# Loading Exponential's table behind ScalarE's first two copies instead of ahead of them

## Chip, cores and metric

The kernel runs on one core of a Trainium2 chip. The metric is device time in microseconds (us), the median over runs of the same program; smaller is better.

## What is computed

Routed attention is followed by a gated feed-forward layer. Batch is 4, there are 8 heads, 768 tokens, 64 numbers a head, 16 clusters a head, and a feed-forward width of 1536. Cut to what matters, the reference is:

```python
c_n = centroids / norm(centroids)              # per head, 16 clusters
q_assign = argmax(q_n . c_n); k_assign = argmax(k_n . c_n)
mask   = q_assign[..., :, None] == k_assign[..., None, :]
scores = where(mask, scale * q k^T, -1e9)
attn   = softmax(scores)                       # scale = 1/8
x      = (attn v) as [3072, 512]
xn     = x / sqrt(mean(x*x) + 1e-6) * rms_g
out    = (silu(xn @ w_gate) * (xn @ w_val)) @ w_out
```

## The kernel before

The work is cut into eight units: a batch and half of its queries (384). Inside a unit, each of the eight heads has three steps of scores; a step is two matmuls of 128 keys by 384 queries (L348) and one Exponential over 128 by 768 on ScalarE (L352). The product with the values follows one head later (`pv`, L366); after every second head VectorE divides (L371, L373). The feed-forward layer of a unit is woven into the attention of the next.

The order on every engine is written out by hand (`manual_schedule`), and each engine runs its list strictly in that order; semaphores make it wait for the others. So a late instruction delays all that stands behind it on its engine.

The mask is made inside the score matmul. Each head's keys and queries are extended by rows that hold a one in the row of the token's own cluster (tiles `kext` and `qext`, 64 rows of numbers and 16 of clusters). For the first heads they are prepared thus, and this document calls the key and query of head n "key n" and "query n":

1. `trans(g, h, part)`: TensorE transposes the loaded float32 tile in three matmuls into PSUM (tile `tq`, L221, one of three buffers), and a copy brings it to SBUF (tile `qkT`): by ScalarE (L227), or by VectorE where `on` is `nc.vector` (L225). `part` 1 is the key, 0 the query.
2. `casts(pool_, n, ...)`: GpSimd (POOL) casts `qkT` to bfloat16 into `kext` and `qext` (L240), in halves of the tokens: K0 and K1 of the key, Q0 and Q1 of the query.
3. `pair_clusters`: TensorE multiplies with the normalised centroids (tile `cblk`) into `sc` (L320), VectorE transposes (L323, `scT`), takes the maximum (L326, `mx`) and compares (L327, `pads`).
4. `head(n)`, that is `under`: VectorE transposes the compared tile into the cluster rows (L332), key first, then query.

POOL also casts the values (`vcast`, L243, tile `vbf`) and issues the loads of the weights (L204). The beginning of POOL's list is: K0, Q0, K1 of head 0; K0, Q0, K1 of head 1; K0, K1, Q0 of head 2; the same of head 3; Q1 of heads 0 and 1; the value cast of head 0; the first two weight loads; the value cast of head 1; Q1 of heads 2 and 3; the value casts of heads 2 and 3; K0, K1, Q0 of head 4.

The beginning of TensorE's list is: key 0, the transpose of the centroids (`c_ps`, L192), query 0, key 1, the clusters of head 0, query 1, key and query 2, the clusters of head 1, key and query 3, key 4, and then the scores of head 0. The first product with the values stands behind the second score step of head 1, and behind it stand the transposes of key and query 7, a score step, and the clusters of heads 4 and 5.

The centroids' norms are made by ScalarE's Sqrt (L182), and ScalarE's functions need their table: the profile shows an ACT_TABLE_LOAD ahead of Sqrt, one ahead of the first Exponential, and one ahead of the first Silu near the end. `first_exp` (L184) is an Exponential of 128 numbers whose output nobody reads; it stands where the table is to be loaded. `off` is a constant that POOL wrote at the start.

Of the kernel before, what the change touches and what calls it, by code (L numbers as in the profile page):

```python
# [14 lines left out]
ACT = mybir.ActivationFunctionType  # L15
# [7 lines left out]
def kernel(  # L23
# [12 lines left out]
    nc = tc.nc  # L36
# [135 lines left out]
    off = const.tile([P, 1], F32)  # L172
# [8 lines left out]
    c_norm = const.tile([P, 1], F32)  # L181
    nc.scalar.activation(c_norm, c_ss, ACT.Sqrt)  # L182
    first_exp = const.tile([P, 1], F32)
    nc.scalar.activation(first_exp, off, ACT.Exp)  # L184
    c_inv = const.tile([P, 1], F32)
    nc.vector.reciprocal(c_inv, c_norm)
    nc.vector.tensor_scalar_mul(c_n[:, :D], c_in, c_inv)
# [2 lines left out]
    def centroids_t():  # L190
        c_ps = ps_s.tile([P, P], F32, tag="s", name="c_ps")
        nc.tensor.transpose(c_ps, c_n, ident_f)  # L192
        nc.vector.tensor_copy(cblk[:D, :, :NC], c_ps[:D].rearrange("d (h c) -> d h c", c=NC))
        nc.vector.tensor_copy(cblk[D:, :, NC:], c_ps[D:].rearrange("d (h c) -> d h c", c=NC))
# [17 lines left out]
    def trans(g, h, part, on=None):  # L212
        if (g, h // 2) not in qkT:
            qkT[g, h // 2] = qk32.tile([P, 2, 2, UQ], F32, tag="qkT", name="qkT")
        qk = staged[g * HG + h]
        if g * HG + h >= BH:
            nc.vector.transpose(qkT[g, h // 2][:, h % 2, part], qk[:, part].rearrange("p t d -> p (t d)"))
            return
        ps = ps_g.tile([P, UQ], F32, tag="gen", name="tq")
        for i in range(HT):  # L220
            nc.tensor.transpose(ps[:, i * P:(i + 1) * P], qk[:, part, 2 * i:2 * i + 2].rearrange("p t d -> p (t d)"),  # L221
                                ident_f)
        to, by = qkT[g, h // 2][:, h % 2, part], 1.0 / ZS if part and g < BG else 1.0
        if on is nc.vector:
            nc.vector.tensor_scalar_mul(to, ps, by)  # L225
        else:
            nc.scalar.activation(to, ps, ACT.Copy, scale=by)  # L227
# [84 lines left out]
    def pair_clusters(p, heads=(0, 1)):  # L312
        g, h = divmod(2 * p, HG)
        what = [(h + i, m) for i in heads for m in range(2)]
        at = [slot(2 * p + i, m) for i in heads for m in range(2)]
        r = slice(min(at), max(at) + 32)
        pool = ps_g if p else ps_s
        ps = pool.tile([P, UQ], F32, tag="gen" if p else "s", name="sc")
        for a, (hh, m) in sorted(zip(at, what)):
            nc.tensor.matmul(ps[a:a + 32], lhsT=cblk[:, g * HG + hh], rhs=qkT[g, hh // 2][:, hh % 2, m],  # L320
                             start=True, stop=True)
        sct = asg.tile([P, UQ], F32, tag="scT", name="scT", bufs=2)
        nc.vector.transpose(sct[r], ps[r])  # L323
        cl = sct[r].rearrange("p (b e c) -> p b e c", e=2, c=NC)
        mx = small.tile([P, NB, 2], F32, tag="mx", name="mx")[r]
        nc.vector.tensor_reduce(mx, cl, axis=AX, op=ALU.max)  # L326
        nc.vector.tensor_tensor(pads[p][r, :, :NC].rearrange("p b c e -> p b e c"), cl,  # L327
                                mx.unsqueeze(3).broadcast_to([mx.shape[0], NB, 2, NC]), op=ALU.is_equal)
# [234 lines left out]

    K0, K1, Q0, Q1 = (1, 0), (1, 1), (0, 0), (0, 1)
    pool_ = nc.gpsimd
    trans(0, 0, 1, nc.vector)
    centroids_t()
    trans(0, 0, 0)
    trans(0, 1, 1)
    pair_clusters(0, (0,))  # L570
    casts(pool_, 0, K0, Q0, K1)
# [173 lines left out]
```

## Time and profile before

| | before |
|---|---|
| median of 3 runs | 327.1 us (326.96 to 327.35) |
| profiled execution | 327.35 us, of which the span is 325.6 |
| PE (TensorE matmul) busy | 317.8 us, 98% of the span |
| ACT (ScalarE) busy | 245.6 us, 75% |
| DVE (VectorE) busy | 219.8 us, 68% |
| POOL (GpSimd) busy | 137.9 us, 42% |
| granted TensorE clock | 1.00 in every stage |

All times of instructions are in us from the start of the span. A row of the timeline gives start, duration, engine, line, operation, output<-input, shapes, the number of merged instructions and, in brackets, how long the engine had sat idle and what ended that. A row of the windows gives a stretch, its length, and for each engine its busy time and, in brackets, its instructions. The chain of waits is followed back from the end of the stretch that is asked for.

### The profile page before, as it was taken

The numbers are of one execution on the slowest core, as the hardware profiler recorded it, in microseconds if no ns is written. First come the engines' busy times: TensorE is split into PE (matmuls) and PEld (weight loads), VectorE is DVE, ScalarE is ACT, GpSimd is POOL, SyncE is SP. The second block draws the span as 40 slices with busy tenths as digits, with TensorE's granted clock in tenths as the row PEclk, the third lists the DMA queues.
The fourth block names the chain that finished last, engine by engine and source line by source line (L and its number), as shares of the span: only waits on it lengthen the run. The fifth ranks groups of instructions, "written<-read, shape, count | busy, mean of one in ns | idle before, by whom it ended". The sixth has DMA issues, their size and how long they took to land.

```text
span 325.6 us, 7766 instructions
## 1 busy us (share of the span) xinstructions
PE 317.8 (98%) x2839; PEld 190.8 (59%) x2853; DVE 219.8 (68%) x502; ACT 245.6 (75%) x424; POOL 137.9 (42%) x277
## 2 busy tenths in 40 slices
PE   8999899999999999999999999999999999999996
PEld 4546656655556655665566555665566656654654
DVE  5999977989578676878677685876265645682430
ACT  5899988977769867897778866798779868862322
POOL 6999499998726265440916257350000000000000
PEclk9999999999999999999999999999999999999999
DMA  7999995997546644561555540000700040004002
GB/s 256 372 274 226 201 178 102 162 182 147 98 74 158 133 101 74 119 155 53 98 92 127 149 113 34 6 21 1 148 2 0 2 113 34 0 2 133 15 1 97
DMA packets 90310, 34.63 MB, mean 106 GB/s; under 512 B 71968, under 2 KB 87200, under 8 KB 90272
## 3 DMA queue, kind: packets, MB, share of 16 engines
q1 hardware_dynamic: 81104, 27.84, 36.6%
q0 software_dynamic: 8880, 5.91, 10.9%
q8 instruction: 22, 0.36, 0.4%
q10 hardware_dynamic: 288, 0.39, 0.4%
q14 instruction: 16, 0.13, 0.1%
HBM read 28.61 MB, written 6.29 MB: 107 GB/s over the span
## 4 chain that ended last, share of the span: by engine, by line
PE 85%; DVE 10%; ACT 2%; issue 1%; DMA 1%; DVEq 0%; ACTq 0%
PE gate L442 18%; PE val L442 18%; PE o L467 18%; PE s L348 17%; PE acc L366 9%; PE sc L254 3%; DVE kext L332 1%; DVE qext L332 1%; DVE pads L327 1%; DMA boot<-in_centroids_dram 1%; DVE x L373 1%; PE o L478 1%; ACT pT L352 1%; DVE qkT L225 1%; DVE xn L391 1%
## 5 line engine op out<-in xcount | busy, mean ns | idle before, releaser
L352 ACT ACTIVATE pT<-s,off 128x768 bf16<-128x768 f32 x192 | 170.9, 904 | 30.9 <-PE s L348 30.1
L348 PE MATMUL s<-qext,kext 80*128 80x384 bf16 x384 | 94.9, 328 | 1.6 <-ACT pT L352 0.8
L442 PE MATMUL gate<-xnT,wg 128*128 128x384 bf16 x384 | 78.4, 326 | 0.2
L442 PE MATMUL val<-xnT,wv 128*128 128x384 bf16 x384 | 78.2, 326 | 0.0
L451 DVE SCALAR_TENSOR_TENSOR th<-th,gate 128x384 f32<-128x384 f32 x81 | 44.6, 551 | 33.6 <-ACT th L450 32.9
L467 PE MATMUL o<-wo,gvT 128*128 128x512 bf16 x262 | 66.0, 379 | 0.8
L348 PEld LDWEIGHTS <-kext 80*128 80x128 bf16 x384 | 36.4, 98 | 35.1 <-issue 7.5
L455 DVE SCALAR_TENSOR_TENSOR gvT<-th,val 128x384 bf16<-128x384 f32 x81 | 44.5, 550 | 9.4 <-PE val L442 3.9
L442 PEld LDWEIGHTS <-wg 128*128 128x128 bf16 x384 | 36.1, 97 | 23.6 <-issue 1.1
L240 POOL CAST qext<-qkT 64x384 bf16<-64x384 f32 x64 | 35.6, 563 | 32.5 <-DVE inv L371 19.2
L366 PEld LDWEIGHTS <-pT 128*128 128x128 bf16 x1152 | 43.4, 97 | 10.1 <-DVE x L373 1.0
L450 ACT ACTIVATE th<-gate 128x384 f32<-128x384 f32 x81 | 39.7, 490 | 12.3 <-PE gate L442 11.5
L442 PEld LDWEIGHTS <-wv 128*128 128x128 bf16 x384 | 35.7, 97 | 22.6 <-DMA qext<-oh 0.6
L366 PE MATMUL acc<-vbf,pT 128*128 128x65 bf16 x1152 | 45.7, 193 | 0.6 <-ACT pT L352 0.2
L467 PEld LDWEIGHTS <-gvT 128*128 128x128 bf16 x276 | 26.0, 97 | 26.1 <-issue 0.2
L297 POOL DMA_DIRECT2D qext<-oh x48 | 23.1, 492 | 29.5 <-DVE oh L286 29.5
L240 POOL CAST kext<-qkT 64x384 bf16<-64x384 f32 x58 | 31.4, 541 | 4.3 <-DVE qkT L225 2.4
L470 ACT COPY o_sb<-o 128x512 f32<-128x512 f32 x23 | 13.5, 585 | 17.6 <-PE o L467 17.6
L297 POOL DMA_DIRECT2D kext<-oh x48 | 23.1, 488 | 8.1 <-DVE oh L286 7.8
L371 DVE RECIPROCAL inv<-acc 128x6 f32<-128x6 f32 x32 | 6.0, 188 | 23.7 <-PE acc L366 23.2
L373 DVE TENSOR_TENSOR x<-acc,inv 128x384 f32<-128x384 f32 x32 | 17.8, 558 | 1.1
L453 DVE TENSOR_TENSOR gvT<-th,val 128x384 bf16<-128x384 f32 x15 | 8.2, 554 | 14.7 <-PE val L442 8.2
(79 smaller groups left out, 238.4 us busy)
## 6 DMA issues: line engine op xcount, KB each, us to landing
vs<-in_v_dram SPq DMA_DIRECT2D x32, 192.0 KB, 4.0
out_dram<-o_sb SPq DMA_DIRECT2D x23, 256.0 KB, 2.5
qk<-in_q_dram SPq DMA_DIRECT2D x72, 48.0 KB, 2.6
qk<-in_k_dram SPq DMA_DIRECT2D x72, 48.0 KB, 2.5
qk<-in_q_dram SPq DMA_DIRECT2D x14, 192.0 KB, 4.1
qk<-in_k_dram SPq DMA_DIRECT2D x12, 192.0 KB, 4.2
wg<-in_moe_w_gate_dram POOLq DMA_DIRECT2D x4, 384.0 KB, 8.9
wv<-in_moe_w_val_dram POOLq DMA_DIRECT2D x4, 384.0 KB, 10.4
```

Source lines behind the costliest of these rows:

```text
L240: on.tensor_copy(to, of)
L297: on.dma_start(out=ext[D:D + NC, h, e * UQ:(e + 1) * UQ], in_=put[g, m][32 * h + e * NC:32 * h + (e + 1) * NC])
L348: nc.tensor.matmul(ps[:, j, :w] if nt == HT else flat[:, j * w:(j + 1) * w], lhsT=cols(kext[g % 4][:KR, hh], g, kc // HT, kc % HT * P, (kc ...
L352: nc.scalar.activation(pT[u, h][:, n * i:n * i + n, :w], of, ACT.Exp, bias=off, scale=scale if g >= BG else scale * ZS)
L366: nc.tensor.matmul(acc[:, h % 2, t], lhsT=pT[u, h][:, kc, t * P:(t + 1) * P], rhs=vbf[g % 4][:, hh, kc % HT * 2 + kc // HT], start=kc == 0 ...
L373: nc.vector.tensor_tensor(dst, acc[:, :, :nt, :D], inv[:, :, :nt].unsqueeze(3).broadcast_to([P, 2, nt, D]), op=ALU.mult)
L442: nc.tensor.matmul(ps, lhsT=w[:, c, f * P:(f + 1) * P], rhs=xnT[u][:, c, :n], start=c == 0, stop=c == CC - 1)
L450: nc.scalar.activation(th, ps, ACT.Tanh, scale=0.5)
L451: nc.vector.scalar_tensor_tensor(th, th, 1.0, ps, op0=ALU.add, op1=ALU.mult)
L455: nc.vector.scalar_tensor_tensor(gvT[u][:, f, :n], gates[u], 0.5, ps, op0=ALU.mult, op1=ALU.mult)
L467: nc.tensor.matmul(outs[u], lhsT=gvT[u][:, f, t * P:(t + 1) * P], rhs=wo[:, f], start=f == 0, stop=f == FC - 1)
L470: nc.scalar.copy(o, outs[u])
```

## The change

The tiny Exponential is taken away from its place behind Sqrt and put behind query 0's `trans`. Key 0's copy, which VectorE did (L225), is done by ScalarE. ScalarE's list was: Sqrt, table load, `first_exp`, the copies of query 0, key 1, query 1, ... It is now: Sqrt, the copies of key 0 and query 0, table load, `first_exp`, the copies of key 1, query 1, ...

```diff
@@ -181,7 +181,6 @@
     c_norm = const.tile([P, 1], F32)
     nc.scalar.activation(c_norm, c_ss, ACT.Sqrt)
     first_exp = const.tile([P, 1], F32)
-    nc.scalar.activation(first_exp, off, ACT.Exp)
     c_inv = const.tile([P, 1], F32)
@@ -563,9 +562,10 @@
     pool_ = nc.gpsimd
-    trans(0, 0, 1, nc.vector)
+    trans(0, 0, 1)
     centroids_t()
     trans(0, 0, 0)
+    nc.scalar.activation(first_exp, off, ACT.Exp)
     trans(0, 1, 1)
     pair_clusters(0, (0,))
     casts(pool_, 0, K0, Q0, K1)
```

## The prediction

> **What bounds the kernel now.** I read the busy time by stretch first, to see where a delay at the start could still be lost.
>
> ```profile
> 8.00:15.00 7.00, 6.55 (x48) 3.77 (x47) 6.60 (x11) 5.90 (x13) 6.60 (x12) 1.00 1.04 370
> 36.40:40.40 4.00, 3.21 (x37) 2.02 (x35) 3.62 (x14) 4.00 (x8) 0.00 (x0) 1.00 1.21 221
> 50.00:150.00 100.00, 99.66 (x924) 60.13 (x928) 76.22 (x171) 80.97 (x144) 61.77 (x125) 1.00 0.65 126
> ```
>
> Columns: PE, PEld, DVE, ACT, POOL. From 50 on PE is full, so nothing late is made up there. In 8 to 15 DVE and POOL are busy 6.60 of 7.00 each. What the start costs is paid once, 1:1, at the end; the edit lies wholly in it. Next, ScalarE's timeline and the chain of waits to 40 us:
>
> ```profile
> 4.35 1.28 ACT L184 ACT_TABLE_LOAD   x1
> 5.65 0.20 ACT L184 ACTIVATE first_exp<-off 128x1 f32<-128x1 f32 x1
> 5.75 0.86 ACT L227 ACTIVATE qkT<-tq 128x384 f32<-128x384 f32 x2
> 7.69 1.25 ACT L227 ACTIVATE qkT<-tq 128x384 f32<-128x384 f32 x3 [1.07 <-PE tq L221]
> ```
> ```profile
> 5.85 0.40 ACT qkT L227
> 6.25 0.09 issue
> 6.34 0.85 PE sc L320 x4
> ```
>
> The chain runs through the table load to query 0's copy and the first cluster product; from 7.22 it is nearly all VectorE. Last, POOL's and PE's timelines:
>
> ```profile
> 6.97 1.28 POOL L240 CAST kext<-qkT 64x384 bf16<-64x384 f32 x2
> 8.24 0.61 POOL L240 CAST qext<-qkT 64x384 bf16<-64x384 f32 x1
> 8.92 2.10 POOL L240 CAST kext<-qkT 64x384 bf16<-64x384 f32 x3
> ...
> 13.09 1.80 POOL L240 CAST qext<-qkT 64x384 bf16<-64x384 f32 x3
> 14.95 0.50 POOL L243 CAST vbf<-vs 128x384 bf16<-128x384 f32 x1
> ```
> ```profile
> 15.51 0.71 PE L366 MATMUL acc<-vbf,pT 128*128 128x65 bf16 x18
> 17.17 0.85 PE L320 MATMUL sc<-qkT,cblk 128*32 128x384 f32 x8
> ```
>
> POOL hardly idles from 6.97 to 36.40, and its value cast ends at 15.46, 0.05 before PE's first value product. That product waits for POOL; anything that makes POOL late there makes PE late.
>
> **The table's way out of the chain: 0.** Query 0's copy starts at 5.75 behind `first_exp`. But its third transpose on PE starts at 5.44 and takes 0.27: 5.71. A copy starts 0.04 behind its transpose (7.65 to 7.69), so 5.75 again. The chain names ScalarE, but PE is late by the same amount: PE waits for the centroids (DVE L188, to 4.98). The cluster product stays at 6.34.
>
> **Key 0's copy: 0.** Key 0's transposes end at 4.80; ScalarE copies from 4.84 to 5.32 (0.48, L227). DVE loses 0.55 at 4.90 to 5.45. Its copies of `cblk` end 0.08 sooner, at 6.01, where query 0's copy ends at 6.23. DVE then idled 1.13 up to 7.22, so its saving is worth nothing.
>
> **The table's new place.** The load starts 0.02 behind query 0's copy: 6.25 to 7.53; `first_exp` 7.54; key 1's copy 0.11 behind: 7.65 to 8.13, before 6.13 to 6.62. ScalarE had 1.07 idle here and 0.65 before 9.60. Query 1 follows at 8.04 (0.39 apart as now), key 2 at 8.41; query 2's transpose needs key 1's PSUM buffer: copy 8.78 for 8.45. PE's product for head 1's clusters needs query 1: 8.59 for 8.24, ends 9.43; VectorE takes it at 10.55. Key 4's copy ends 11.19 for 10.85, and the first Exponential starts at 11.20, bound by a score that ends at 11.17. ScalarE and PE are on time again: 0. The cover is VectorE's chain, 1.1 deep at head 1's clusters, but only 0.01 at the first Exponential: what came later than reckoned there would be paid 1:1.
>
> The Trainium skill (ScalarE: Activation LUTs, What ACT_TABLE_LOAD costs) gives 1.28 us for the load and 1.38 for a drain, 2.66 per switch. Here Sqrt ended at 4.33 and `first_exp` began at 5.65, 1.32 for all, so the trace decides; by the page key 1 would come 1.4 later still, and the loss below grow by about as much.
>
> **POOL.** Its cast of key 1 starts 0.06 behind the copy (6.24 to 6.30): 8.19 for 7.65, so 0.55 late. Query 1's cast was itself held by its copy; two like halves overlap by 0.08 (13.75, 14.28), so it starts at 8.73 for 8.24: 0.48 late. This is the least POOL is behind.
>
> **Casts against compares.** POOL's casts disturb DVE's compares (L327), and the other way:
>
> ```profile
> L327 DVE TENSOR_TENSOR pads<-scT,mx x5: 604/835/853, 8.4 to 24.7; 128x384 bf16<-128x384 f32 x3, 64x384 bf16<-64x384 f32 x2
> ```
>
> Alone a compare takes 0.60. One that starts under a cast ends 0.39 behind that cast (8.86 to 9.24, 12.21 to 12.60), 0.43 behind a value cast (19.80 to 20.24). A cast that starts under a compare ends 0.45 behind it (12.26 to 13.05; 0.61 alone). Replaying the list by these rows:
> - Compare 1 (8.40): key 1's cast ends 8.80, compare 9.19 (9.24 before). Query 1's cast ends 9.64 for 8.86. The four casts behind it run 0.06, 0.06, 0.04, 0.04 apart: POOL is 0.62 late, and query 2's cast is 11.68 to 12.29.
> - Compare 2 starts at 11.70, just behind that cast: ends 12.68 (+0.08). Key 3's K0 ends 13.13, K1 13.78 (13.05): 0.73 late. Q1 of head 1: 15.01 to 15.62.
> - Compare 3 (15.12) ends 16.03 (+0.13). The value cast starts at 15.69 under it and ends 0.35 behind it (0.51 long alone, so 0.10 less than the others): 16.38 for 15.46. The first value product: 16.43, 0.92 late.
> - PE runs without a gap from there to the cluster product of heads 4 and 5, which ends at 18.95 for 18.03. DVE takes it at 18.98 for 18.41: **+0.57**. DVE was free at 18.38, so 0.35 of PE's lateness is hidden; that is the only cover.
> - The two weight issues lose the stretch of the first (0.90, 0.77; 0.75 alone), so POOL is 0.78 late: the last value cast ahead of compare 4 is 20.08 to 20.58, and compare 4, from 20.19, ends 21.01 for 20.24: **+0.20**, since it fell clear before (0.62). Compare 5 meets the end of a cast as before: 0.
>
> DVE is then busy to the norm (L410, ends 40.37), whose output opens PE's full stage. Sum: 0.57 + 0.20 = **+0.77**.
>
> The unknown is who gets ahead, and it can fall below this. If no cast or compare is stretched otherwise than now, POOL is 0.48 late, PE's product ends 18.51, DVE starts 18.55: +0.14. If compare 2, which starts only 0.02 behind the cast, gets ahead: it ends at 12.30, the cast at 12.75, POOL is 0.89 late, the value cast behind compare 3 ends 16.68, DVE is 0.87 late and, with compare 4, 1.07. I take 0.77, which follows most rows, and keep 0.14 and 1.07. Of the later pairs (DVE casts at 27.33 of 0.37 and 0.69, a square at 33.61 of 0.91 where others take 0.55) either sign is possible, up to 0.68.
>
> The Trainium skill (SBUF, Who interferes with whom) says that a two-input VectorE instruction and a GpSimd read exclude each other for the whole instruction. The compares show a lock but a softer one: 12.21 to 12.60 is 0.39 and not the whole 0.60. By the page compare 3 would end near 16.2, the value cast near 16.7, and the sum be some 0.35 larger.
>
> **Rivals.** *Lag only* (+0.14): the casts are just shifted. For it: PE and ScalarE recover by 11.2. Against it: a cast shifted by half its length meets another stretch of the compare. 327.25.
>
> *Casts fall clear of the compares*, the other side. Three compares take 0.83 to 0.85 for 0.60. At 18.41 DVE can gain only if the value cast is under 0.35 late: POOL must win back over 0.13 of its 0.48; its stretched casts (0.78 and 0.80 for 0.61) hold 0.36, so at most 0.23 is gained there. With the later pairs (0.68) the end is -0.91; half of it is 326.65. Against it: key 1's cast runs when compare 1 starts, by the arithmetic above.
>
> *Copy brings a load of its own*, so that the edit does not do what it says: no copy of this trace runs behind Sqrt's load. Then the load stays at 4.35, key 0's copy starts at 5.65, query 0's ends 6.52 for 6.24, the cluster product 0.28 later, and POOL's key 1 cast at 8.07: +0.3 to +0.8, 327.6.
>
> **How the numbers follow.** The profiled execution took 327.35: span 325.6 and 1.75 around it; it is the slowest of the three runs, 0.25 over the median. 327.35 + 0.77 - 0.25 = 327.87. About 0.2%, 0.65 us, is what a measurement of this kernel can tell from no change. The forecast (+0.4 to +1.1) has 0.68: over 0.65 in 0.54, under in 0.14. Lag only 0.18 (same). Casts clear 0.10 (0.06 faster, 0.04 same). Own load 0.04 (half slower). Slower 0.56, same 0.38, faster 0.06. Range: below, most of the clear case, -0.4, 326.7; above, 1.07 and half of the later pairs, 328.5.
>
> **What would show it.** Right: a table load at 6.25, the cluster product still at 6.34, POOL's key 1 cast at 8.19, the value product near 16.4, VectorE's transpose near 19.0, the norm's last row ending near 41.1. Wrong: a first cluster product before 6.2, a fourth table load, the value product before 15.9, or the compares' median under 0.7.

## The result and the profile after

The changed kernel takes 328.41 us (median of 6 runs, 327.82 to 328.92) against 327.27 us for the kernel before on the same chip (6 runs, 326.96 to 327.36): ratio 1.0034, 95% interval 1.0021 to 1.0047. It is slower by 1.14 us by the medians. The profiled execution took 328.92 us with a span of 327.1, the longest of the six, so its trace shows more of the loss than the median does.

Line numbers behind L183 are one less than before (the score matmul is L347, the value product L365, the compare L326). The busy time by stretch, in the columns PE, PEld, DVE, ACT, POOL, first one row of the kernel before and then two of the changed kernel:

```profile
15.00:20.00 5.00, 4.58 (x61) 2.72 (x59) 4.67 (x9) 5.00 (x9) 4.87 (x9) 1.00 1.10 339
```
```profile
15.00:20.00 5.00, 3.63 (x42) 2.04 (x40) 3.60 (x7) 3.67 (x8) 4.87 (x8) 1.00 1.03 358
50.00:150.00 100.00, 99.66 (x928) 59.98 (x934) 76.47 (x169) 80.72 (x140) 63.26 (x129) 1.00 0.66 126
```

From 15 to 20 us PE, DVE and ACT fall to some 3.6 of 5.00; before they were busy 4.58, 4.67 and 5.00 there. Only POOL is as busy as before (4.87 both times). From 50 on nothing is different. ScalarE's timeline shows the table's new place and what comes behind it:

```profile
4.84 0.49 ACT L226 ACTIVATE qkT<-tq 128x384 f32<-128x384 f32 x1 [0.60 <-PE tq L220]
6.10 0.49 ACT L226 ACTIVATE qkT<-tq 128x384 f32<-128x384 f32 x1 [0.78 <-PE tq L220]
6.61 1.28 ACT L568 ACT_TABLE_LOAD   x1
7.91 0.20 ACT L568 ACTIVATE first_exp<-off 128x1 f32<-128x1 f32 x1
8.02 1.61 ACT L226 ACTIVATE qkT<-tq 128x384 f32<-128x384 f32 x4
```

Key 1's copy starts at 8.02, before at 6.13. The copies at 4.84 and 6.10 run behind Sqrt's table without a load between; the Trainium skill (ScalarE: Activation LUTs, Table sets: the hidden batching unit) lists copy among the functions of every set, and the trace agrees. From the chain of waits to 24 us, in time and without its rows of "issue" (0.05 at most), and the two rows of PE that matter:

```profile
14.99 1.45 POOL qext L239 x2
16.50 0.51 POOL vbf L242
17.05 0.71 PE acc L365 x18
```
```profile
17.05 0.71 PE L365 MATMUL acc<-vbf,pT 128*128 128x65 bf16 x18 [1.37 <-POOL vbf L242]
18.72 0.85 PE L319 MATMUL sc<-qkT,cblk 128*32 128x384 f32 x8
```

The chain now runs through POOL, which it did not touch before. The first value product waits 1.37 us for POOL's value cast and starts at 17.05 instead of 15.51; the cluster product of heads 4 and 5 follows at 18.72 instead of 17.17. VectorE's division after it (`x`) starts at 23.31, before at 21.75, and the 1.56 us between them stay to the end.

```profile
8.55 0.62 POOL L239 CAST kext<-qkT 64x384 bf16<-64x384 f32 x1 [0.62 <-ACT qkT L226]
9.08 0.92 POOL L239 CAST qext<-qkT 64x384 bf16<-64x384 f32 x1
10.06 1.95 POOL L239 CAST kext<-qkT 64x384 bf16<-64x384 f32 x3
12.05 1.04 POOL L239 CAST qext<-qkT 64x384 bf16<-64x384 f32 x1
14.34 2.10 POOL L239 CAST qext<-qkT 64x384 bf16<-64x384 f32 x3
```
```profile
8.76 0.79 DVE L326 TENSOR_TENSOR pads<-scT,mx 64x384 bf16<-64x384 f32 x1
12.05 0.61 DVE L326 TENSOR_TENSOR pads<-scT,mx 64x384 bf16<-64x384 f32 x1
15.11 0.88 DVE L326 TENSOR_TENSOR pads<-scT,mx 128x384 bf16<-128x384 f32 x1
```

POOL waits 0.62 us for key 1's copy, and then two casts of query halves take 0.92 and 1.04 where one alone takes 0.61: one started under compare 1, the other together with compare 2. The three casts from 14.34 take 2.10 together, before 1.80: the last of them meets compare 3. So a lateness of 0.90 at 8.55 has become 1.55 at the value cast (16.50 against 14.95).

### The profile page after: what moved, and what is told of

The parts are those of the page before. It is cut to its first block, busy times and chain, and to the rows that moved or that the text cites. A ratio compares the mean times of both kernels' runs of the same rounds, so it can differ in the third digit from the quotient of the medians.

```text
span 327.1 us, 7765 instructions
## 1 busy us (share of the span) xinstructions
PE 318.8 (97%) x2839; PEld 191.4 (59%) x2853; DVE 219.4 (67%) x501; ACT 246.0 (75%) x425; POOL 138.5 (42%) x277
## 4 chain that ended last, share of the span: by engine, by line
PE 86%; DVE 7%; ACT 4%; issue 1%; DMA 1%; POOL 1%; DVEq 0%; ACTq 0%
PE gate L441 18%; PE val L441 18%; PE o L466 18%; PE s L347 17%; PE acc L365 9%; PE sc L253 3%; ACT pT L351 1%; ACT qkT L226 1%; PE tq L220 1%; DVE x L372 1%; DMA boot<-in_centroids_dram 1%; PE o L477 1%; DVE qkT L224 1%; DVE xn L390 1%; DVE xn L409 1%
## 5 line engine op out<-in xcount | busy, mean ns | idle before, releaser
L347 PE MATMUL s<-qext,kext 80*128 80x384 bf16 x384 | 94.9, 328 | 1.1 <-ACT pT L351 0.8
L347 PEld LDWEIGHTS <-kext 80*128 80x128 bf16 x384 | 36.4, 98 | 34.7 <-issue 7.5
L239 POOL CAST qext<-qkT 64x384 bf16<-64x384 f32 x64 | 36.6, 579 | 33.0 <-DVE inv L370 19.2
L365 PEld LDWEIGHTS <-pT 128*128 128x128 bf16 x1152 | 43.4, 97 | 11.3 <-issue 1.6
L365 PE MATMUL acc<-vbf,pT 128*128 128x65 bf16 x1152 | 45.7, 193 | 1.8 <-POOL vbf L242 1.4
L216 DVE STREAM_TRANSPOSE qkT<-qk 128x384 f32<-128x384 f32 x36 | 18.1, 548 | 0.1
```

The source lines that it names most:

```text
L239: on.tensor_copy(to, of)
L347: nc.tensor.matmul(ps[:, j, :w] if nt == HT else flat[:, j * w:(j + 1) * w], lhsT=cols(kext[g % 4][:KR, hh], g, kc // HT, kc % HT * P, (kc ...
L365: nc.tensor.matmul(acc[:, h % 2, t], lhsT=pT[u, h][:, kc, t * P:(t + 1) * P], rhs=vbf[g % 4][:, hh, kc % HT * 2 + kc // HT], start=kc == 0 ...
```

## The experiments

Each was timed beside the kernel before, which took 327.33 us (33 runs, 326.89 to 327.85) in the first four experiments and 327.40 us (30 runs, 326.86 to 328.32) in the others.

**The table load alone**, key 0's copy back on VectorE:

```diff
-    trans(0, 0, 1)
+    trans(0, 0, 1, nc.vector)
```

> The changed kernel with key 0's copy back on VectorE; only the table load stays behind query 0's copy. Theory A (the late table makes key 1's copy late, POOL's casts with it, and POOL then holds the first value product): key 0's copy is worth nothing, so 328.4 us as the changed kernel, between 328.0 and 328.8, with the first value product near 17. Theory B (key 0's copy on ScalarE is what costs): 327.3 as before.

Measured: 328.21 us (327.79 to 328.40), ratio 1.0024 (1.0015 to 1.0033): +0.88, within theory A's bounds, far from theory B's. Its profiled execution (328.30 us) had the same start as that of before (first cluster product at 6.33), so it is the one to lay beside it. The first value product starts at 16.45. From the chain of waits, in time:

```profile
6.25 1.28 ACT L568
7.54 0.20 ACT first_exp L568
7.75 0.39 ACT qkT L226
8.19 0.62 POOL kext L239
8.81 0.84 POOL qext L239
...
15.73 0.67 POOL vbf L242
16.45 0.71 PE acc L365 x18
17.15 0.69 PE tq L220 x6
17.84 0.34 PE s L347 x2
18.18 0.83 PE sc L319 x8
19.03 0.59 DVE scT L322
19.65 0.56 DVE mx L325
20.24 0.95 DVE pads L326
```

It is one chain: the table, key 1's copy, POOL's casts (left out are the casts between and the rows of "issue", of at most 0.06), the value cast, the value product, the clusters of heads 4 and 5, VectorE. The division `x` starts at 22.69 here and at 21.75 before: +0.94.

**Key 0's copy alone** on ScalarE, the table load behind Sqrt as before:

```diff
-    trans(0, 0, 1, nc.vector)
+    trans(0, 0, 1)
```

> The kernel before with key 0's copy on ScalarE and the table load left behind Sqrt. Theory A: key 0's copy now waits for the load (5.65 us), query 0's copy ends 6.5 and the first cluster product starts 0.3 later than 6.34; POOL's cast of key 1 about 0.4 late: 327.6 to 328.1. Theory B (key 0's copy on ScalarE is the whole cost): 328.4.

Measured: 327.38 us (327.32 to 327.49), ratio 0.9998 (0.9989 to 1.0007): no difference. Theory B falls, and the loss that theory A expected didn't come either. ScalarE's timeline of the profiled execution shows how key 0's copy went there:

```profile
3.87 1.28 ACT L184 ACT_TABLE_LOAD   x1
5.17 0.20 ACT L184 ACTIVATE first_exp<-off 128x1 f32<-128x1 f32 x1
5.28 1.38 ACT L227 ACTIVATE qkT<-tq 128x384 f32<-128x384 f32 x3
```

The centroids had arrived half a microsecond sooner than in the profile of before, so the load stood at 3.87 and not at 4.35, and query 0's transposes ran at half their rate: the copy of key 0 found room ahead of query 0's. No profile with late centroids was taken. The eleven runs lie within 0.17 us of each other, the kernel before's within 0.96, and the fastest, 327.32, is only as fast as the median before: it may be that the copy costs something where the centroids come early and nothing where they come late. That stays open; what the runs show is that the medians don't differ.

**Key 1's copy by VectorE**, on top of the change:

```diff
-    trans(0, 1, 1)
+    trans(0, 1, 1, nc.vector)
```

> The changed kernel with key 1's copy by VectorE, which idles there: POOL's cast of key 1 no longer waits for the table. Theory A: POOL is on time, the first value product near 15.5 to 15.9, and the time is that of before, 327.1 to 327.5. Theory C (ScalarE's other copies behind the load, and PE's transposes that wait for them, are the cost): query 1, key 2 and query 2 still come late, so it stays at 328.0 or more.

Measured: 327.10 us (326.89 to 327.54), ratio 0.9992 (0.9984 to 1.0001). One copy of 0.56 us, moved to an engine that idled, takes back the whole loss. The table load is still behind query 0's copy. But the run doesn't test theory C as was meant: with key 1's copy gone from ScalarE, query 1, key 2 and query 2 are copied from 7.21 on, before from 7.69, in an execution that began 0.48 sooner (first cluster product 5.86 for 6.34), so they aren't late any more. Against theory C speaks the table-only run: its copies behind the load are late, yet its first Exponential starts at 11.17, before at 11.20, so ScalarE had lost nothing by then. POOL's timeline:

```profile
6.50 1.30 POOL L239 CAST kext<-qkT 64x384 bf16<-64x384 f32 x2
7.77 0.61 POOL L239 CAST qext<-qkT 64x384 bf16<-64x384 f32 x1
8.44 2.11 POOL L239 CAST kext<-qkT 64x384 bf16<-64x384 f32 x3
...
14.52 0.50 POOL L242 CAST vbf<-vs 128x384 bf16<-128x384 f32 x1
```

There is no wait in it from 6.50 on, and it has the pattern of before, 0.45 us sooner throughout because the centroids were early in this execution.

**Head 3's casts behind the first value cast**, on top of the change:

```diff
-    casts(pool_, 3, K0, K1, Q0)
     trans(1, 0, 1)
     casts(pool_, 0, Q1)
     casts(pool_, 1, Q1)
     vcast(0)
+    casts(pool_, 3, K0, K1, Q0)
```

> The changed kernel with POOL's three casts of head 3 moved behind the first value cast, so that Q1 of heads 0 and 1 and the value cast come about 2 us sooner. Theory A: neither PE nor ScalarE waits for POOL there any more, though POOL's casts of key 1 are as late as in the change; 327.2 to 327.7. Theory C (ScalarE's and PE's own lateness): no change, 328.4.

Measured: 327.80 us (327.31 to 328.28), ratio 1.0012 (1.0003 to 1.0021). About half of the loss comes back, a little less than expected. The profile shows the value product at 15.70, and PE and ScalarE don't wait for POOL from 7 to 26 us, so the mended place is mended; ScalarE's copies behind the load are as late as in the changed kernel (from 8.04 on), and yet about half of the loss is gone, which speaks against theory C too. The execution began 0.38 late (first cluster product 6.72 for 6.34), and the division `x` is no later than that (22.09, before 21.75). VectorE then loses 0.46 more further on, in the squares:

```profile
32.57 0.65 DVE L390 SCALAR_TENSOR_TENSOR xn<-x 128x384 bf16<-128x384 f32 x1
33.62 0.92 DVE L390 SCALAR_TENSOR_TENSOR xn<-x 128x384 bf16<-128x384 f32 x1
34.47 0.90 DVE L390 SCALAR_TENSOR_TENSOR xn<-x 128x384 bf16<-128x384 f32 x1
```

Before they took 0.55, 0.55 and 0.91: one more meets a cast of POOL's. PE waits for POOL again at 26.40 and 26.87 and ScalarE at 35.91, by 0.5 us at most. This is one execution; how much of the 0.47 in the median is due to it was not separated.

**The value cast alone sooner**, on top of the change:

```diff
+    vcast(0)
     casts(pool_, 0, Q1)
     casts(pool_, 1, Q1)
-    vcast(0)
```

> The changed kernel with POOL's first value cast moved ahead of Q1 of heads 0 and 1, so 1.2 us sooner; the two Q1 casts, which free the tile that ScalarE's copy of key 6 writes, come 0.5 us later. If PE's first value product alone carries the loss: 327.4 to 327.8. If ScalarE's copy of key 6, behind which Exponentials and key 7 are queued, carries it as well: little or nothing comes back, 328.2 to 328.8.

Measured: 328.51 us (328.06 to 328.89), ratio 1.0031 (1.0018 to 1.0043): nothing comes back. PE's first value product starts at 15.50, on time, but ScalarE stands still:

```profile
16.82 0.49 ACT L226 ACTIVATE qkT<-tq 128x384 f32<-128x384 f32 x1 [1.71 <-POOL qext L239]
17.21 0.90 ACT L351 ACTIVATE pT<-s,off 128x768 bf16<-128x768 f32 x1
18.00 0.49 ACT L226 ACTIVATE qkT<-tq 128x384 f32<-128x384 f32 x1
```

Key 6's copy writes the `qkT` tile of heads 0 and 1 (there are three such tiles), and that is free only when POOL has cast Q1 of both. Exponentials stand behind it. So POOL's lateness reaches the clusters of heads 4 and 5 on two ways. The run doesn't show that they are equally long, since the last Q1 cast also ends 0.36 later here than in the changed kernel. An estimate from the rows: here the cluster product starts 1.77 behind key 6's copy (18.59 and 16.82); with key 6's copy at 16.47, as in the changed kernel, that gives 18.24, where by way of the value product it was 18.72 and before 17.17. The second way alone would carry some 1.07 of the 1.55.

**The maximum of compares 1 and 2 in PSUM**, on top of the change, so that a compare has one SBUF input instead of two:

```diff
-        mx = small.tile([P, NB, 2], F32, tag="mx", name="mx")[r]
+        if p == 0:
+            room = ps_a.tile([P, 512], F32, tag="acc", name="mx_ps")
+            mx = room[:, :2 * NB].rearrange("p (b e) -> p b e", e=2)[r]
+        else:
+            mx = small.tile([P, NB, 2], F32, tag="mx", name="mx")[r]
```

> The changed kernel with the maximum of compares 1 and 2 in PSUM instead of SBUF, so that a compare has one SBUF input. Theory A with the lock (casts and two-input compares hold each other up, and that turns POOL's 0.5 us into 0.9): compares 1 and 2 take 0.60 to 0.65 and no cast about them over 0.65; the value product comes 0.4 sooner than in the table-only run and the time is 327.4 to 327.9. Without the lock (POOL's lateness alone): compares and casts as before, 328.2 to 328.4.

Measured: 327.56 us (327.13 to 328.00), ratio 1.0005 (0.9996 to 1.0013). That is 0.16 over the kernel before, where the changed kernel was 1.14 over it, though POOL's cast of key 1 starts as late as in the changed kernel (8.55 in both profiles). The first value product starts at 16.22, 0.23 sooner than in the table-only run, though this execution began 0.36 later. VectorE's compares and POOL's casts:

```profile
8.90 0.58 DVE L330 TENSOR_TENSOR pads<-scT,mx_ps 64x384 bf16<-64x384 f32 x1
12.01 0.60 DVE L330 TENSOR_TENSOR pads<-scT,mx_ps 64x384 bf16<-64x384 f32 x1
```
```profile
9.08 0.62 POOL L239 CAST qext<-qkT 64x384 bf16<-64x384 f32 x1
9.76 1.96 POOL L239 CAST kext<-qkT 64x384 bf16<-64x384 f32 x3
11.76 0.63 POOL L239 CAST qext<-qkT 64x384 bf16<-64x384 f32 x1
```

The casts that took 0.92 and 1.04 take 0.62 and 0.63, and the value cast starts at 15.51 instead of 16.50, with the same overlaps: the cast at 9.08 starts under compare 1, and compare 2 at 12.01 under a cast. The stretch comes from the two SBUF inputs, and it is what makes a late cast expensive.

**The same in the kernel before:**

> The kernel before with the maximum of compares 1 and 2 in PSUM. With the lock and VectorE's chain as the bound of the start: compares 1 and 2 lose 0.23 and 0.25 us, 326.8 to 327.0. If VectorE isn't the bound there, or the lock isn't what stretches them: 327.3.

Measured: 327.10 us (326.86 to 327.58), ratio 0.9989 (0.9980 to 0.9998): -0.30, less than the 0.48 that the two compares lost. VectorE now comes early to the clusters of heads 4 and 5 and waits for PE there:

```profile
17.68 0.58 DVE L323 STREAM_TRANSPOSE scT<-sc 128x384 f32<-128x384 f32 x1 [0.50 <-PE sc L320]
18.88 0.94 DVE L331 TENSOR_TENSOR pads<-scT,mx 128x384 bf16<-128x384 f32 x1
```

In this execution, which began 0.46 sooner (first cluster product 5.88), the division `x` comes 0.41 sooner (21.34, before 21.75), so the gain was lost again by then.

This run is the one to lay beside the run above, since it has the same compares. The change costs 327.56 - 327.10 = 0.46 on top of it, and 1.14 with all compares reading SBUF twice: some 0.7 us of the loss goes with the inputs of compares 1 and 2, by medians whose intervals reach 0.3 to 0.4 us to either side. The traces are sharper. From the kernel before to the changed one, POOL's lateness grew from 0.90 at key 1's cast to 1.55 at the value cast. From this run to the run above it is 1.35 at key 1's cast (8.55 for 7.20) and 1.29 at the value cast (15.51 for 14.22): a lateness is passed on and doesn't grow.

**Key 1 by VectorE and the maximum of compares 1 to 3 in PSUM**, on top of the change (`p < 2` in place of `p == 0`):

> The changed kernel with key 1's copy by VectorE and the maximum of compares 1, 2 and 3 in PSUM: neither the late key 1 nor the stretch of the first three compares. Theory A with the lock: 0.23, 0.25 and 0.25 us under the run with key 1 by VectorE, 326.4 to 326.7, faster than before. Without the lock: 327.1 to 327.3.

Measured: 327.03 us (326.59 to 327.34), ratio 0.9985 (0.9977 to 0.9994): a little faster than the kernel before, but 0.07 under the run with key 1 by VectorE, which is within their spread, and so outside theory A's bounds. The compares do what theory A says (0.58, 0.60 and 0.58), and VectorE is done 0.74 sooner with what stands ahead of the clusters of heads 4 and 5 (17.64 for 18.38). There it waits 0.18 for the cluster product, and compare 4, which has two SBUF inputs still, takes 0.94 for 0.62: at the division `x` 0.26 is left (21.49 for 21.75). Whether compare 4 with one SBUF input would keep the rest was not measured.

## Why the prediction was right, step by step

*The table's way out of the chain, 0.* Right: the first cluster product is at 6.33 in the table-only run for 6.34 before. *Key 0's copy, 0.* The medians agree: alone it takes 327.38 us for 327.33, and behind a late table the difference isn't clear of the spread (see the size). In the changed kernel's own profile the first cluster product is at 6.69 and not at 6.34, because query 0's transposes were slow there (see the last section).

*POOL's cast of key 1 at 8.19.* Right to the digit in the table-only run, whose start is that of the profile before. In the changed kernel's own profile it is 8.55, 0.36 of it from the late start.

*Casts against compares.* The replay gave 0.98 for compare 2, a value cast ending at 16.38, a value product at 16.43 and VectorE at 18.98. The table-only run has 1.00 (the longest of its five compares), 16.40, 16.45 and 19.03:

```profile
L326 DVE TENSOR_TENSOR pads<-scT,mx x5: 596/886/1002, 8.4 to 25.7; 128x384 bf16<-128x384 f32 x3, 64x384 bf16<-64x384 f32 x2
```

In the changed kernel's own profile compare 2 and the cast start together (12.05 each) and the compare gets ahead: 0.61 and 1.04. That was the prediction's upper case, +1.07; with 0.36 from the start it makes most of the +1.56 of that execution. The switch between the two cases is a matter of some 0.03 us, and the traces show both: where compare 2 starts 0.03 or 0.02 behind the cast (the table-only run; head 3's casts later, 12.10 and 12.07) it takes 1.00 and 0.99, where they start together (the changed kernel; the value cast sooner) it takes 0.61 and 0.60. How often each comes isn't known. That casts and compares keep their length in the same overlaps once a compare has one SBUF input shows the lock as the cause of the stretch.

*The rivals.* Lag only (+0.14) and casts that fall clear of the compares are refuted by the table-only run: +0.88, with compares as long as above. A load ahead of the copy is refuted by ScalarE's timeline: the copies at 4.84 and 6.10 have none ahead of them, and the changed kernel has three table loads as before.

*The size.* +0.77 was forecast, 327.87 us; measured was 328.41. The kernel before itself came out at 327.27 instead of 327.1, which is 0.17 of the difference; the rest is a loss of +1.14, a little above the +0.4 to +1.1 that the prediction held likely and close to its upper case. The table-only run has +0.88 in the median and +0.94 in its trace. The term that was mis-sized there is compare 4: 0.94 long, not 0.82, so +0.32 and not +0.20 over its 0.62 of before:

```profile
19.62 0.62 DVE L327 TENSOR_TENSOR pads<-scT,mx 128x384 bf16<-128x384 f32 x1
```

Behind it stands a step on POOL: the prediction had the two weight issues, 0.90 and 0.77 long, fall back to 0.75 and so win back 0.14 of POOL's lateness. They take 0.90 and 0.76 again; the value cast under which compare 4 starts ends at 20.74, not at 20.58, and the compare 0.44 behind it. The term of VectorE's start at the clusters was +0.62 for +0.57. The changed kernel's +1.14 is 0.26 more than the table alone, but the ranges of the two overlap; whether key 0's copy adds anything behind a late table isn't shown. The later pairs, for which the range allowed half of 0.68 to either side, changed nothing: the two casts of VectorE's and the squares are as long in the changed kernel's profile as before. So the mechanism was right, and that the time lies within the range owes something to a width put there for another reason.

*What was missed.* The prediction had one way from POOL to the clusters of heads 4 and 5, the value product. Key 6's copy is a second one, and for that reason the value cast moved ahead gave nothing back. By the estimate above it is the shorter one in the changed kernel, so that it didn't spoil the number.

*The cover.* It was put at 0.35, DVE's lead at the clusters of heads 4 and 5. In the table-only run the cluster product starts 0.94 later than before (18.11 for 17.17) and VectorE 0.62 later: 0.32.

The Trainium skill (SBUF, Who interferes with whom) has it that a VectorE instruction with at most one SBUF input, outside its 2-port modes, does not contend with GpSimd. The run with the maximum in PSUM agrees: 0.58 and 0.60 under running casts. Its whole-instruction lock is harder than what the compares show, 0.39 behind a cast where 0.60 is their full length.

## What to carry to other kernels

Before a wait is moved off the chain, look at when its successor's own input arrives: the table load was on the chain by name, but PE was late by the same amount, so moving it gave nothing. Then follow what is queued behind its new place, and whom that feeds: here a copy that nobody on the old chain waited for fed POOL, an engine without slack. Where two engines disturb each other, a shift of half a microsecond can end as nearly a whole one (0.54 at key 1's cast and 0.94 at the value product in the table-only run); a compare with one input in PSUM took the disturbance away.

## What was not expected of the hardware

Executions begin differently, in stretches that no edit touched. The centroids were used by VectorE at 3.14 in one profile and at 3.62 in that of before. TensorE's early transposes started 0.11 apart in some executions from 4.7 us on, and in others 0.21 apart until 6.3 (changed kernel):

```profile
5.21 1.50 PE L220 MATMUL tq<-ident_f,qk 128*128 128x128 f32 x6
```

The same six took 0.82 in the profile of before. Both moved the first cluster product, between 5.86 and 6.72 us across the profiles, which is as much as the table load alone costs. It may be part of why runs of one kernel differ by 0.2 to 1.5 us here, but only one execution of each kernel was profiled. The wide spacing at query 0's transposes was seen in five of the ten profiles, all five with key 0's copy on ScalarE (seven profiles), none of the three with it on VectorE. By ten single executions that can be chance or a cost of the change that the prediction doesn't have; it stays open.

The Trainium skill (TensorE: Matmul & The Clock Gate, Part 1) has a clock that steps up after a free-running window of activity, so that the step falls differently from run to run; the two spacings fit that. The column of the granted clock shows 1.00 in these stretches and does not show the step.
